# Attention, feed-forward and soft mixture-of-experts on one core: weight loads on a second queue, and a new order of the first sixteen tiles

## Chip, cores and metric

The kernel runs on 1 core of one Trainium2 chip. The metric is the device time of one execution in microseconds (us), shorter is better. The engines have short names: PE (TensorE matmul), PEld (its weight loads), DVE (VectorE), ACT (ScalarE), POOL (GpSimd), SP (SyncE, which here only issues DMAs).

## What is computed

The reference runs three stages over 4 batches of 768 positions (3072 tokens, 512 wide):

```python
# 1 local attention, 8 heads of 64, blocks of 32, window 16
k_sum = k.reshape(B, H, nb, block, D).max(axis=3)
v_sum = v.reshape(B, H, nb, block, D).mean(axis=3)
# scores against the near keys (masked) and against all k_sum (+ log(block)), one softmax over both
attn = softmax(concat(local, summary)) @ concat([v, v_sum])
# 2 feed-forward on x = attn, 3072 x 512, d_ff 2048
h = x @ w_in
x = (h * np.cos(h)) @ w_out
# 3 soft mixture of experts, 8 experts x 4 slots
logits = x @ phi
slot_input = softmax over tokens(logits).T @ x
out = softmax over slots(logits) @ (relu(slot_input @ w1) @ w2)
```

## The kernel before

**Tiles.** Stage 2 is a loop of 96 tiles, s = 0 to 95: 6 blocks of 512 tokens, each with 16 slices f = s % 16 of 128 hidden columns. Tile s does `mm1(s)` (lines 347 to 351: h = x·w_in in three passes of high and low parts), then the cosine (lines 365 to 372 on DVE, line 367 on ACT), the split of the product in a high part `gh` (line 375, ACT) and a low part `gl` (line 376, POOL), and two tiles later `mm2(s)` (lines 388 to 392). The low part of `w_in` (line 336, `wil`) is made by DVE for the first 16 slices and by POOL later; that of `w_out` (`wol`) always by POOL; both high parts (line 335) by ACT.

**Weights.** They come as 8-byte integers. In the first 16 tiles each slice is loaded once (`load_w`, line 113, 1 MB) and converted: `conv_1` (lines 123 and 127, ACT), `conv_2` (line 133, a shift on DVE), `conv_3` (line 138, an add on POOL). From f = 4 the load of slice f + 2 goes into the buffer which the conversion of slice f has just read.

**Attention.** Groups g = 0 to 3 are done before the tile loop; 4 to 7 fall into tiles 0 to 15, the others later. A group is: `att_K` (line 227, ACT copies the maxima of the keys in), `att_A` (line 250 PE scores `sc`, line 254 DVE scale and mask), `att_max` and `att_sub` (lines 262, 266), `att_exp` for two groups (line 271, ACT, with a load of another function table before it and one after it), `att_sum`, `att_norm` (lines 276, 290 to 293, DVE), `att_C` twice (line 300 PE transposes `tr`, line 306 copies `aT`), `att_D` (line 317 `av`, line 326). `HB` gives the half tile in which the groups of the second batch begin, (2, 13) for groups 4, 5 and 6, 7. The scores, transposes and value means of these groups share two PSUM banks (`ps_m`).

**Second batch's maxima and means.** Four loads of keys (`load_kraw`, line 162, buffer `kr`), each reduced by DVE (line 167, `ks`), and three of values (`load_vb`, line 174, `vb`), each averaged on PE (line 181, `vs`) and added by DVE (lines 190, 192), all through one buffer: each load waits for the reader of the one before. Load i stands at the end of tile i, its reader at the end of tile i + 1 (`at(i, 1, load)`, `at(i + 1, 1, use)`).

**Order.** Inside `manual_schedule` each engine runs its instructions in the order in which the code writes them. In a tile: mm1, lines 365 to 367, the attention pieces of position 0 (`fire(s, 0)`), lines 372 to 376, mm2 of tile s - 2, the low part for tile s + 2, the shift and add of slice s + 3 (`convert`, parts 2), the high and low part of `w_out`, `conv_1` of slice s + 4, the pieces of position 1. All DMAs are issued by SP, in this order too.

Of the kernel before, what the change touches and what calls it, by code (L numbers as in the profile page):

```python
# [12 lines left out]
I32 = mybir.dt.int32  # L13
# [13 lines left out]
KL = QB + 2 * WIN  # L27
NSUM = S // SUMB
KC = KL + NSUM
# [16 lines left out]
WARM1 = 4  # L46
WARM2 = 4
NRING = 7
HB = (2, 13)
HF = (-6, 10)  # L50
OA = 4
OV = 3
# [22 lines left out]
def body(ctx: ExitStack, tc: tile.TileContext, q0, qk, kT, vn, vx, w, phi, ex, cst, out):  # L75
    nc = tc.nc
# [30 lines left out]

    raw = {}

    def load_w(f):  # L110
        pool, tag, n = {2: (xres, "xl", 2), 3: (xres, "xh", 2)}.get(f, (m2, ("x2", "x2T")[f % 2], 1))
        raw[f] = pool.tile([128, 2, 512, 2], I32, name=f"raw{f}", tag=tag, bufs=n)
        return nc.sync.dma_start(out=raw[f].rearrange("p a c t -> p (a c t)"), in_=w[f].bitcast(I32))

    def conv_1(f, parts=(0, 1)):

# [14 lines left out]
    def conv_2(f):  # L131
        wi_ = W[f].rearrange("p a c -> p (a c)").bitcast(I32)
        nc.vector.tensor_single_scalar(out=wi_, in_=wi_, scalar=3, op=ALU.logical_shift_left)

    def conv_3(f):

        wi_ = W[f].rearrange("p a c -> p (a c)").bitcast(I32)
        return nc.gpsimd.tensor_tensor(out=wi_, in0=wi_, in1=cvt.pop(f), op=ALU.add)  # L138


    ksums, vsums, grp = {}, {}, {}
# [3 lines left out]
    def bank(name):  # L145

        pool, tag = banks[turns[0] % len(banks)]
        turns[0] += 1
        return pool.tile([128, 512], F32, name=name, tag=tag)
# [4 lines left out]
    def load_kraw(n):  # L154
        if n < 4:
            t = wres.tile([128, WIN + S + WIN], F32, name=f"kr{n}", tag=f"w{12 + n}")
            nc.gpsimd.memset(t[:, 0:WIN], 0.0)
            kfirst.append(t)
            t = t[:, WIN:WIN + S]
        else:  # L160
            t = att.tile([128, S], F32, name=f"kr{n}", tag="v2", bufs=1)
        nc.sync.dma_start(out=t, in_=kT[n])
        ksums[n] = t
# [30 lines left out]
    def vsum_first():  # L194

        ps = bank("vs0")
        for i in range(3):
            vsum_mm(ps, 0, i, i == 0, i == 2)
        vsums[0] = m2.tile([128, 4, 128], F32, name="vs0", tag="sacc")
        for p in range(4):  # L200
            nc.vector.tensor_copy(vsums[0][KL:KL + 32, p, :], ps[32 * p:32 * p + 32, 0:128])
# [11 lines left out]
    def load_v(g):  # L213
        pool, tag = {2: (wres, "w7"), 3: (att, "qk")}.get(g, (att, "v"))
        t = grp[g]["v"] = pool.tile([128, 2, 4, 128], F32, name=f"v{g}", tag=tag)
        nc.sync.dma_start(out=t.rearrange("p j w c -> p (j w c)"), in_=vx[g])

    def load_vs(g):
        p = 2 * (g % 2)
        for j in range(2):  # L220
            vs = vsums[0][KL:KC, p + j, :] if g < 6 else vsums[g // 6][32 * (p + j):32 * (p + j) + NSUM, :]
            nc.sync.dma_start(out=grp[g]["v"][KL:KC, j], in_=vs.unsqueeze(1).to_broadcast([NSUM, 4, 128]))
# [36 lines left out]
    def att_max(g, negate=False):  # L259
        d = grp[g]  # L260
        d["mx"] = stat.tile([128, 8], F32, name=f"mx{g}", tag="mx")
        nc.vector.tensor_reduce(out=d["mx"], in_=d["S"], axis=AX.X, op=ALU.max, negate=negate)
# [23 lines left out]
    def att_norm(g, eng=None):  # L286

        d = grp[g]
        sm = d["sm"]
        nc.vector.tensor_scalar(out=sm, in0=sm, scalar1=1e-9, scalar2=W_SCALE * TWO_PI, op0=ALU.add, op1=ALU.mult)  # L290
        rs = stat.tile([128, 8], F32, name=f"rs{g}", tag="rs")
        nc.vector.reciprocal(out=rs, in_=sm)
        (eng or nc.vector).tensor_tensor(out=d["S"], in0=d["S"],  # L293
                                         in1=rs.unsqueeze(2).to_broadcast([128, 8, KC]), op=ALU.mult)

    def att_C(g, j, eng=None):
        d = grp[g]
        ps = bank(f"tr{g}_{j}") if g < 4 else ps_m.tile([128, 512], F32, name=f"tr{g}_{j}", tag="m")
        for u in range(4):
            nc.tensor.transpose(ps[:KC, 128 * u:128 * u + 128], d["S"][:, 4 * j + u, :], ident)  # L300
        if g < 4:
            pool, tag, n = ring, ("gh", "gh", "gh", "gl", "gl", "gl", "a", "a")[2 * g + j], 2 if g == 3 else 3
        else:
            pool, tag, n = att, "aT", 2
        aT = pool.tile([KC, 512], F32, name=f"aT{g}_{j}", tag=tag, bufs=n)
        (nc.vector.tensor_copy if eng is nc.vector else nc.scalar.copy)(aT, ps[:KC, :])
        d["aT", j] = aT

    def att_D(g):
        d = grp[g]  # L310
        ps = bank(f"av{g}") if g < 4 else ps_m.tile([128, 512], F32, name=f"av{g}", tag="m")
        for j in range(2):
            for u in range(4):
                c = 256 * j + QB * u
                for hh in range(2):
                    r = slice(64 * hh, 64 * hh + 64)
                    product = nc.tensor.matmul(ps[r, c:c + QB], d["v"][:KC, j, u, r],  # L317
                                               d["aT", hh][:, 256 * j + QB * u:256 * j + QB * u + QB], start=True, stop=True)
        b, o = g // 4, 256 * ((g // 2) % 2)
        if b not in xh:  # L320
            xh[b] = xres.tile([128, 4, TB], F32R, name=f"xh{b}", tag="xh", bufs=2)
            xl[b] = xres.tile([128, 4, TB], F32R, name=f"xl{b}", tag="xl", bufs=2)
        p = 2 * (g % 2)
        ps = ps.rearrange("p (j c) -> p j c", j=2)
        hi, lo = (x[b][:, p:p + 2, o:o + 256] for x in (xh, xl))
        return product, nc.scalar.copy(hi, ps), nc.vector.tensor_tensor(out=lo, in0=ps, in1=hi, op=ALU.subtract)  # L326
# [174 lines left out]
    def at(s, pos, fn, *a):  # L501
        bg.setdefault((s, pos), []).append((fn, a))
# [12 lines left out]
    def fill(n):  # L515

        for i in range(n):
            nc.tensor.matmul(warmth[:, 0:128], ones, ones, start=True, stop=True)
# [4 lines left out]
    def scores(g):  # L523
        att_A(g)
        att_max(g, True)

    def turn(g, eng=None):
        for j in range(2):
            att_C(g, j, eng or nc.vector)
# [37 lines left out]
    att_norm(2, nc.gpsimd)  # L567
    scores(3)
    vsum_first()
    for g in (0, 2, 1, 3):  # L570
        load_vs(g)
    load_w(2)
    load_qk(4)
    load_w(3)
    att_exps(3)
    att_norm(1, nc.gpsimd)
    fill(8)
    turn(0)
    fill(6)
    conv_1(0)  # L580
    load_w(4)
    conv_1(1)
    load_w(5)
    turn(2)
    att_norm(3, nc.gpsimd)
    fill(8)
    turn(1)
    conv_2(0)
    conv_3(0)
    att_D(0)  # L590
    fill(4)
    turn(3, nc.scalar)
    att_D(2)
    split_w(0, 0, nc.vector)
    conv_2(1)
    conv_3(1)
    att_D(1)
    att_D(3)
    load_qk(5)
    load_v(4)  # L600
    load_v(5)
    load_vs(4)
    load_vs(5)
    split_w(1, 0, nc.vector)
# [5 lines left out]
    def convert(f, parts):  # L610
        if 1 in parts and f < NF:
            conv_1(f)
            if 4 <= f < NF - 2:
                load_w(f + 2)
        if 2 in parts and f < NF:
            conv_2(f)
            conv_3(f)


    for g in range(4, 24):  # L620
        h0 = HF[g // 2 % 2] + 2 * NF * (g // 4 - 1) if g > 7 else HB[g // 2 % 2]
        h = h0 + OA * (g % 2)
# [20 lines left out]
        else:  # L643
            v = n - 14 + OD2
# [15 lines left out]
    for b in range(1, B):  # L660
        s = 8 * (3 * b - 2) - 4
        for i in range(7):
            load, use, k = (load_kraw, ksum, (4 * b + i,)) if i < 4 else (load_vb, vsum, (b, i - 4))
            if b == 1:
                at(i, 1, load, *k)
                at(i + 1, 1, use, *k)
            else:
                at(s - 22 + 2 * i, 1, load, *k)
                at(s - 20 + 2 * i, 0, use, *k)
# [28 lines left out]
    for s in range(NSLOT + LAG):  # L698
        if s < NSLOT:
            mm1(s)  # L700
            if s == 0:
                convert(2, (2,))
            act1(s)
        fire(s, 0)
        if s < NSLOT:
            act2(s)
        if s >= LAG:
            mm2(s - LAG)
            if (s - LAG) % NF == NF - 1:
                last = [x2_out(t) for t in range(4)][3]  # L710
        if s == 0:
            convert(3, (1,))
        if s + 2 < NSLOT:
            split_w((s + 2) % NF, 0, nc.vector if s + 2 < NF else None)
        convert(s + 3, (2,))
        if s < NSLOT:
            split_w(s % NF, 1)
        convert(s + 4, (1,))
        fire(s, 1)
        fire(s, 2)  # L720
        if s - LAG >= NSLOT - NF:
            grab(wres, f"w{s - LAG - (NSLOT - NF)}")
# [129 lines left out]
    for h in range(2):  # L852
        c = slice(256 * h, 256 * h + 256)
# [22 lines left out]
        for i in range(NB):  # L876
            pool, tag, kw = places[(NB * h + i) % 4]
            o = pool.tile([128, 4, 256], F32, name=f"o{h}_{i}", tag=tag, **kw)
            for t in range(2):
# [3 lines left out]
                for n in range(2):  # L883
                    k = 512 * (i % 2) + 256 * t + 128 * n
# [78 lines left out]
```

## Time and profile before

| | us |
|---|---|
| time, median of 2 runs | 805.51 (805.39 to 805.64) |
| the profiled execution's own time | 806.3 |
| its span in the trace | 804.5 |

The profile gives, for each engine, when each instruction started, how long it ran, and how long the engine stood idle before it, with what released it. Times in the rows count from the span's start. In what follows a tile is dated by the start of its first DVE instruction, line 365.

### The profile page before, as it was taken

How to read it: one execution, taken by the hardware profiler on the slowest of the kernel's cores; microseconds unless marked ns; L12 is line 12 of the kernel's file. 1: busy time of each engine (PE TensorE's matmuls, PEld its weight loads, DVE VectorE, ACT ScalarE, POOL GpSimd, SP SyncE). 2: the span in 40 equal slices, each digit the busy share in tenths (PEclk: the TensorE clock that was granted, in tenths of full speed). 3: DMA queues.
4: the chain of work that ended last, by engine and by line, in shares of the span. 5: the costliest groups of instructions: out<-in, count | busy, mean ns of one | idle time of the engine just before them, and what ended most of it. 6: DMA issues, size and time to landing. Idle time of an engine off the chain costs nothing.

```text
span 804.5 us, 13755 instructions
## 1 busy us (share of the span) xinstructions
PE 735.0 (91%) x5453; PEld 567.9 (71%) x5453; DVE 476.4 (59%) x692; ACT 395.3 (49%) x703; POOL 412.3 (51%) x304
## 2 busy tenths in 40 slices
PE   8878477768999999999999999999999999999994
PEld 7756356656787788777777776887777888877453
DVE  6557664676656757757566567566576444443623
ACT  5675644733643645545436436455454453633212
POOL 2457454643556565555656565655457676672000
PEclk9999778969999999999999999999999999999998
DMA  9876534304212031041130220210100842227988
GB/s 339 293 271 245 185 143 182 108 20 136 81 50 89 1 115 63 21 141 70 58 106 1 65 76 1 96 43 28 36 1 27 317 155 79 89 94 270 378 313 269
DMA packets 36304, 101.71 MB, mean 126 GB/s; under 512 B 3472, under 2 KB 14736, under 8 KB 34192
## 3 DMA queue, kind: packets, MB, share of 16 engines
q1 hardware_dynamic: 36240, 100.83, 35.3%
q8 instruction: 43, 0.70, 0.4%
q14 instruction: 21, 0.17, 0.1%
HBM read 92.17 MB, written 6.29 MB: 122 GB/s over the span
## 4 chain that ended last, share of the span: by engine, by line
PE 67%; DVE 15%; ACT 7%; DMA 7%; issue 3%; SPq 1%; DVEq 0%; ACTq 0%
PE acc L388 9%; PE h L347 9%; PE h L348 8%; PE acc L389 8%; PE h L351 8%; PE acc L392 8%; DVE S L293 3%; DMA kr<-in_kT_dram 3%; PE av L317 3%; PE tr L300 2%; PE sc L250 2%; DVE a L366 2%; DVE a L365 2%; PE yp L861 2%; ACT S L271 2%
## 5 line engine op out<-in xcount | busy, mean ns | idle before, releaser
L376 POOL TENSOR_TENSOR gl<-a,gh 128x512 fp32r<-128x512 f32 x96 | 125.4, 1306 | 258.2 <-ACT gh L375 228.6
L367 ACT ACTIVATE a<-a,halfpi 128x512 f32<-128x512 f32 x96 | 69.5, 724 | 220.2 <-DVE a L366 211.5
L347 PE MATMUL h<-xh,wih 128*128 128x512 f32 x384 | 160.8, 419 | 5.2 <-ACT wih L335 5.1
L388 PE MATMUL acc<-woh,gh 128*128 128x512 f32 x384 | 159.0, 414 | 1.7 <-ACT gh L375 1.7
L389 PE MATMUL acc<-wol,gh 128*128 128x512 f32 x384 | 153.2, 399 | 3.5 <-POOL wol L336 3.5
L348 PE MATMUL h<-xl,wih 128*128 128x512 f32 x384 | 155.1, 404 | 0.6 <-DVE xl L326 0.6
L365 DVE TENSOR_SCALAR a<-h 128x512 f32<-128x512 f32 x96 | 65.9, 686 | 111.4 <-PE h L351 104.1
L336 POOL TENSOR_TENSOR wol<-w,woh 128x512 fp32r<-128x512 f32 x96 | 130.2, 1356 | 1.4 <-ACT woh L335 1.4
L336 POOL TENSOR_TENSOR wil<-w,wih 128x512 fp32r<-128x512 f32 x80 | 111.8, 1398 | 1.0 <-ACT wih L335 1.0
L375 ACT CAST gh<-a 128x512 fp32r<-128x512 f32 x96 | 59.4, 619 | 95.6 <-DVE a L372 95.5
L351 PE MATMUL h<-xh,wil 128*128 128x512 f32 x384 | 104.8, 395 | 0.0
L392 PE MATMUL acc<-woh,gl 128*128 128x512 f32 x384 | 103.3, 391 | 0.0
L388 PEld LDWEIGHTS acc<-woh,gh 128*128 128x128 f32 x384 | 73.4, 191 | 26.8 <-issue 9.4
L347 PEld LDWEIGHTS h<-xh,wih 128*128 128x128 f32 x384 | 74.8, 195 | 23.8 <-ACT wih L335 6.2
L372 DVE TENSOR_TENSOR a<-h,a 128x512 f32<-128x512 f32 x96 | 65.8, 686 | 39.4 <-ACT a L367 39.4
L389 PEld LDWEIGHTS acc<-wol,gh 128*128 128x128 f32 x384 | 73.6, 192 | 19.7 <-POOL wol L336 4.8
L348 PEld LDWEIGHTS h<-xl,wih 128*128 128x128 f32 x384 | 75.1, 196 | 16.1 <-DVE xl L326 1.0
L351 PEld LDWEIGHTS h<-xh,wil 128*128 128x128 f32 x384 | 72.9, 190 | 17.0 <-POOL wil L336 0.8
L392 PEld LDWEIGHTS acc<-woh,gl 128*128 128x128 f32 x384 | 72.3, 188 | 16.3
L366 DVE SCALAR_TENSOR_TENSOR a<-a,h 128x512 f32<-128x512 f32 x96 | 65.9, 687 | 3.3
L335 ACT CAST woh<-w 128x512 fp32r<-128x512 f32 x96 | 59.2, 616 | 3.0 <-PE acc L392 3.0
L335 ACT CAST wih<-w 128x512 fp32r<-128x512 f32 x96 | 59.1, 616 | 2.6 <-POOL w L138 2.6
(128 smaller groups left out, 879.0 us busy)
## 6 DMA issues: line engine op xcount, KB each, us to landing
ex<-in_ex_dram SPq DMA_DIRECT2D x64, 512.0 KB
raw<-in_w_dram SPq DMA_DIRECT2D x16, 1024.0 KB
qk<-in_qk_dram SPq DMA_DIRECT2D x20, 736.0 KB
v<-in_vx_dram SPq DMA_DIRECT2D x24, 512.0 KB
kr<-in_kT_dram SPq DMA_DIRECT2D x16, 384.0 KB
vb<-in_vn_dram SPq DMA_DIRECT2D x12, 512.0 KB
out_dram<-o SPq DMA_DIRECT2D x12, 512.0 KB
v<-vs SPq DMA_DIRECT2D x48, 48.0 KB
```

The costliest lines, as they stand in the source:

```text
L335: nc.scalar.copy(hi, W[f][:, part, :])
L336: (eng or nc.gpsimd).tensor_tensor(out=lo, in0=W[f][:, part, :], in1=hi, op=ALU.subtract)
L347: nc.tensor.matmul(h, hi[:, c], xh[s // NF][:, t, :], start=t == 0, stop=False)
L348: nc.tensor.matmul(h, hi[:, c], xl[s // NF][:, t, :], start=False, stop=False)
L351: nc.tensor.matmul(h, lo[:, c], xh[s // NF][:, t, :], start=False, stop=t == 3)
L365: nc.vector.tensor_scalar(out=a, in0=h, scalar1=0.25, scalar2=MAGIC, op0=ALU.add, op1=ALU.add)
L366: nc.vector.scalar_tensor_tensor(out=a, in0=a, scalar=MAGIC, in1=h, op0=ALU.subtract, op1=ALU.subtract)
L367: nc.scalar.activation(a, a, AF.Sin, bias=halfpi, scale=-TWO_PI)
L376: nc.gpsimd.tensor_tensor(out=gl, in0=a, in1=gh, op=ALU.subtract)
L388: nc.tensor.matmul(acc[t], gh[:, c], hi, start=f == 0, stop=False)
L389: nc.tensor.matmul(acc[t], gh[:, c], lo, start=False, stop=False)
L392: nc.tensor.matmul(acc[t], gl[:, c], hi, start=False, stop=f == NF - 1)
```

## The change

- `load_w` takes an engine. The loads of slices 4 and up are issued by ACT, right behind the conversion that frees their buffer; those of slices 2 and 3 move ahead on SP.
- `HB` becomes (1, 13): groups 4 and 5 come half a tile earlier; 6 and 7 stay.
- The first `load_kraw` of the second batch stands before the tile loop; the other loads move from position 1 to position 0 of the same tile, the readers from position 1 to 0 of theirs.
- In tiles 1 and up the shift and add of slice s + 3 stand ahead of the low part for tile s + 2. In tile 0 the high part of slice 2 stands ahead of the conversion of slice 3.
- Before the loop, the shift and add of slice 1 stand right behind those of slice 0, and DVE copies the first batch's means for groups 0 and 2 into their values (`copy_vs`) where a DMA did (line 222). Groups 1 and 3 keep the DMA. One `fill` has 6 matmuls for 8.

```diff
-HB = (2, 13)
+HB = (1, 13)
-    def load_w(f):
+    def load_w(f, eng=None):
-        return nc.sync.dma_start(out=raw[f].rearrange("p a c t -> p (a c t)"), in_=w[f].bitcast(I32))
+        return (eng or nc.sync).dma_start(out=raw[f].rearrange("p a c t -> p (a c t)"), in_=w[f].bitcast(I32))
...
+    def copy_vs(g):
+        p = 2 * (g % 2)
+        vs = vsums[0][KL:KC, p:p + 2, :]
+        nc.vector.tensor_copy(grp[g]["v"][KL:KC], vs.unsqueeze(2).to_broadcast([NSUM, 2, 4, 128]))
...
-    for g in (0, 2, 1, 3):
+    load_w(2)
+    load_w(3)
+    for g in (1, 3):
         load_vs(g)
-    load_w(2)
     load_qk(4)
-    load_w(3)
     att_exps(3)
     att_norm(1, nc.gpsimd)
+    copy_vs(0)
...
     conv_1(0)
-    load_w(4)
+    load_w(4, nc.scalar)
     conv_1(1)
-    load_w(5)
+    load_w(5, nc.scalar)
     turn(2)
     att_norm(3, nc.gpsimd)
-    fill(8)
+    copy_vs(2)
+    fill(6)
     turn(1)
     conv_2(0)
     conv_3(0)
+    conv_2(1)
+    conv_3(1)
...
-    conv_2(1)
-    conv_3(1)
...
     load_v(5)
+    load_kraw(4)
...
-                load_w(f + 2)
+                load_w(f + 2, nc.scalar)
...
             if b == 1:
-                at(i, 1, load, *k)
-                at(i + 1, 1, use, *k)
+                if i:
+                    at(i, 0, load, *k)
+                at(i + 1, 0, use, *k)
...
-        if s == 0:
-            convert(3, (1,))
+        if s:
+            convert(s + 3, (2,))
         if s + 2 < NSLOT:
             split_w((s + 2) % NF, 0, nc.vector if s + 2 < NF else None)
-        convert(s + 3, (2,))
+        if s == 0:
+            convert(3, (1, 2))
```

**DVE, tile 1.** `a1` is tile 1's cosine, `S4` the scores of group 4, `mx` and `ks` a maximum of scores and one of keys, `w4` the shift of slice 4, `wil3` the low part for tile 3. Before:

```order
L365 TENSOR_SCALAR a1_682<-h1_669 128x512
L366 SCALAR_TENSOR_TENSOR a1_682<-a1_682,h1_669 128x512
L254 SCALAR_TENSOR_TENSOR S4_686<-sc4_0_687,mask_85 128x480
L254 SCALAR_TENSOR_TENSOR S4_686<-sc4_1_688,mask_85 128x480
L372 TENSOR_TENSOR a1_682<-h1_669,a1_682 128x512
L336 TENSOR_TENSOR wil3_713<-w3_647,wih3_712 128x512
L133 TENSOR_SCALAR w4_661<-w4_661 128x1024
L262 TENSOR_REDUCE mx4_728<-S4_686 128x8
L167 TENSOR_REDUCE ks4_733<-kr4_667 128x24
L365 TENSOR_SCALAR a2_750<-h2_737 128x512
```

With the change (line 254 of group 4 now stands in tile 0):

```order
L365 TENSOR_SCALAR a1_699<-h1_686 128x512
L366 SCALAR_TENSOR_TENSOR a1_699<-a1_699,h1_686 128x512
L262 TENSOR_REDUCE mx4_703<-S4_665 128x8
L167 TENSOR_REDUCE ks4_708<-kr4_603 128x24
L372 TENSOR_TENSOR a1_699<-h1_686,a1_699 128x512
L133 TENSOR_SCALAR w4_659<-w4_659 128x1024
L336 TENSOR_TENSOR wil3_720<-w3_649,wih3_719 128x512
L365 TENSOR_SCALAR a2_748<-h2_735 128x512
```

The two reductions went from the tile's end into its middle, and the shift from behind the low part to before it.

**ACT, tile 6.** `aT4_0` is the copy of group 4's first transposes out of PSUM. Before:

```order
L375 CAST gh6_1022<-a6_1011 128x512
L335 CAST wih8_1038<-w8_920 128x512
L335 CAST woh6_1044<-w6_787 128x512
L123 ACTIVATE w10_1048<-raw10_924 128x1024
L127 ACTIVATE cv10_1050<-raw10_924 128x1024
L367 ACTIVATE a7_1106<-a7_1106,halfpi_90 128x512
L306 COPY aT4_0_1115<-tr4_0_1110 120x512
```

With the change:

```order
L375 CAST gh6_1034<-a6_1013 128x512
L335 CAST wih8_1052<-w8_921 128x512
L335 CAST woh6_1056<-w6_787 128x512
L123 ACTIVATE w10_1060<-raw10_925 128x1024
L127 ACTIVATE cv10_1062<-raw10_925 128x1024
L113 DMA raw12_1064<-in_w_dram 128x2048
L306 COPY aT4_0_1071<-tr4_0_1066 120x512
L367 ACTIVATE a7_1109<-a7_1109,halfpi_90 128x512
```

A weight load stands in ACT's row, and the copy now comes before the next tile's cosine. On PE the scores of group 6 come right behind the transposes `tr4_0` in the new order.

## Rows read from the trace of the kernel before

**Rows 1.** Stretches: us, busy (instructions) of PE, PEld, DVE, ACT, POOL, PEclk, DMA share, GB/s.

```profile
42.00:204.00 162.00, 118.21 (x771) 91.58 (x771) 100.86 (x128) 83.56 (x122) 87.39 (x52) 0.84 0.44 159
204.00:740.00 536.00, 529.42 (x3458) 415.95 (x3459) 324.18 (x466) 270.30 (x467) 312.54 (x238) 1.00 0.23 77
```

**Rows 2.** Timeline of PE (start, us, instruction, idle before it): three long waits.

```profile
89.12 1.08 PE L181 MATMUL vs<-vb,avg 128*32 128x128 f32 x16 [8.23 <-DMA vb<-in_vn_dram]
...
106.59 1.08 PE L181 MATMUL vs<-vb,avg 128*32 128x128 f32 x16 [8.13 <-DVE S L254]
...
128.82 2.11 PE L250 MATMUL sc<-qk 64*64 64x120 f32 x32 [3.92 <-ACT aT L306]
```

**Rows 3.** Timeline of DVE: all of tile 3, up to the start of tile 4.

```profile
67.98 0.68 DVE L365 TENSOR_SCALAR a<-h 128x512 f32<-128x512 f32 x1
68.70 0.69 DVE L366 SCALAR_TENSOR_TENSOR a<-a,h 128x512 f32<-128x512 f32 x1
69.30 1.21 DVE L254 SCALAR_TENSOR_TENSOR S<-sc,mask 128x480 f32<-128x480 f32 x2
70.44 0.68 DVE L372 TENSOR_TENSOR a<-h,a 128x512 f32<-128x512 f32 x1
72.32 1.37 DVE L336 TENSOR_TENSOR wil<-w,wih 128x512 fp32r<-128x512 f32 x1 [1.21 <-ACT wih L335]
73.62 0.68 DVE L133 TENSOR_SCALAR w<-w 128x1024 int32<-128x1024 int32 x1
74.22 1.14 DVE L262 TENSOR_REDUCE mx<-S 128x8 f32<-128x960 f32 x1
...
76.14 0.68 DVE L365 TENSOR_SCALAR a<-h 128x512 f32<-128x512 f32 x1
```

**Rows 4.** Timeline of DVE: the starts of tiles 0, 7, 9 and 11.

```profile
41.97 0.68 DVE L365 TENSOR_SCALAR a<-h 128x512 f32<-128x512 f32 x1
...
112.09 0.69 DVE L365 TENSOR_SCALAR a<-h 128x512 f32<-128x512 f32 x1 [4.06 <-PE h L351]
...
135.62 0.69 DVE L365 TENSOR_SCALAR a<-h 128x512 f32<-128x512 f32 x1 [3.42 <-PE h L351]
...
151.88 0.68 DVE L365 TENSOR_SCALAR a<-h 128x512 f32<-128x512 f32 x1
```

**Rows 5.** Timeline of POOL: the adds of slices 0 and 1, before the loop.

```profile
28.05 2.37 POOL L138 TENSOR_TENSOR w<-w,cv 128x1024 int32<-128x1024 int32 x1 [0.98 <-ACT cv L127]
37.26 2.38 POOL L138 TENSOR_TENSOR w<-w,cv 128x1024 int32<-128x1024 int32 x1 [6.84 <-DVE w L133]
```

**Rows 6.** Timeline of DVE: two products of `att_norm`, POOL idle and POOL busy.

```profile
96.56 1.16 DVE L293 TENSOR_TENSOR S<-S,rs 128x960 f32<-128x960 f32 x1
...
102.89 3.08 DVE L293 TENSOR_TENSOR S<-S,rs 128x960 f32<-128x960 f32 x1
```

**Rows 7.** Timeline of ACT: table load, exponentials, a high part, a conversion.

```profile
82.86 1.28 ACT L271 ACT_TABLE_LOAD   x1
84.15 1.80 ACT L271 ACTIVATE S<-S 128x1920 f32<-128x1920 f32 x1
...
87.27 0.72 ACT L367 ACTIVATE a<-a,halfpi 128x512 f32<-128x512 f32 x1
...
89.79 0.61 ACT L335 CAST woh<-w 128x512 fp32r<-128x512 f32 x1
90.31 1.15 ACT L123 ACTIVATE w<-raw 128x1024 f32<-128x1024 f32 x1
91.37 1.18 ACT L127 ACTIVATE cv<-raw 128x1024 int32<-128x1024 uint32 x1
```

**Rows 8.** Timeline of SP: issues of a means' DMA and of a key load.

```profile
20.79 0.98 SPq L222 DMA_DIRECT2D v<-vs  x1
...
60.70 0.33 SPq L162 DMA_DIRECT2D kr<-in_kT_dram  x1
```

**Rows 9.** Timeline of DVE: the reduction that waited for that key load.

```profile
67.11 0.95 DVE L167 TENSOR_REDUCE ks<-kr 128x24 f32<-128x768 f32 x1 [0.49 <-DMA kr<-in_kT_dram]
```

## The prediction, as put on record before the changed kernel was run

> **What bounds the kernel now.** I first read the stretches [rows 1]. After 204 us PE is busy 529.42 of 536 us at a granted clock of 1.00; nothing in the change touches that part. From 42 to 204 us, in tiles 0 to 15, PE is busy 118.21 of 162 us, and the mean clock is 0.84: its lower level is 1.2 GHz, the upper 2.4. There lie 44 idle us and some slow ones, so only there can this change pay. The timeline of PE then shows who ends the idle time. Three waits alone make 20.3 us [rows 2]: 8.23 on a load of the second batch's values, 8.13 on DVE scaling scores out of PSUM, 3.92 on ACT copying a transpose out of PSUM. None is PE's own, so I read DVE, which has all these tiles' work in one row.
>
> DVE's tile 3 [rows 3] takes 8.16 us from line 365 (67.98) to line 365 of tile 4 (76.14). Its steps, start to start: 1.32 for lines 365 and 366, 1.14 for the scores' scale, 1.88 from line 372 to the low part (of it 1.21 idle for ACT's high part), 1.30 for the low part, 0.60 for the shift, 1.92 for both reductions. PE would need less: 536 us for tiles 16 to 95 is 6.7 per tile, attention included [rows 1]. So the first sixteen tiles go at the pace of DVE's row and of what it waits for, and I price the change tile by tile on that row, then look where PE is later than DVE. Tiles 0, 4, 7, 9 and 11 start at 41.97, 76.14, 112.09, 135.62 and 151.88 [rows 3, 4].
>
> **Before the loop.** POOL's add of slice 1 starts at 37.26 after 6.84 idle, put down to DVE's shift, which stands behind the first low parts [rows 5]. With the shift right behind that of slice 0, the add can follow the first add, which started at 28.05 and took 2.37. Two new copies on DVE delay both. The trace has no such copy. For one, a shift over as many columns gives 0.60 from below, a product held up by POOL 3.08 from above [rows 3, 6]; I take 1.3, nearer the shift, since the copy too has one input. So the add of slice 1 starts at 28.05 + 2.6 + 2.37 = 33.0, and everything up to tile 0 hangs on it: 4.2 us gained; by the bounds 0.7 to 5.7.
>
> **ACT's loads.** No DMA is issued by ACT before. SP's issues take 0.33 for a load and 0.98 for the small means' DMA [rows 8]; I take 0.4, nearer the load, and nothing below zero, since ACT works in order. Twelve make 4.8 us on ACT, which counts only where somebody waits for ACT's tail: tiles 2 and 6 below, inside their sums. In exchange SP's key loads no longer stand behind weight loads. One before took from 60.70 to 67.11, 6.4 us [rows 8, 9]; I take 4.5 and keep 6.4 as the upper bound, and a gain from there is hidden except in tile 2.
>
> The Trainium skill (DMA: Bandwidth & Descriptors, "Issuing engines are not separate DMA queues") speaks against this part: transfers issued by different engines share the same DMA engines, and a second issuer saves only issue time. By it the key loads would keep their 6.4 us and the sum below would be some 2 us smaller; no row before shows two issuers at work.
>
> **Tiles 0 to 3** (34.17 us now). The shift now falls into the 1.21 that DVE waits for ACT, so a plain tile loses 0.60. The cosine needs a table load (1.28) and 0.72 in tile 0 [rows 7].
> - Tile 0: 1.32 + 1.28 + 0.72 + 1.88 + 1.30 + 0.60 + 1.14 (group 4's scale, now here) = 8.2.
> - Tile 1: 1.32 + 1.92 + 1.88 + 1.30 = 6.4. The keys' maxima no longer wait, since their load went out before the loop.
> - Tile 2: ACT's row decides. Behind tile 1's high part come a cast (0.52), the conversion (2.24), the load (0.4), group 5's two key copies (some 0.9, an estimate from two casts) and the cosine 0.72: 4.8, where DVE needs 1.30 + 1.32 + 0.95. So 1.3 of waiting: 1.32 + 0.95 + 1.3 + 1.88 + 1.30 + 1.14 = 7.9. PE's scores of group 5 wait for the same copies; that is hidden behind DVE.
> - Tile 3: 6.4 like tile 1.
>
> Sum 28.9: 5.3 gained.
>
> **Tiles 4 to 6** (35.95 now). Here the earlier attention only moves work.
> - Tile 4: the exponentials now stand before the high part `gh`: 1.32 + 0.72 + 1.28 + 1.80 + 1.04 (two casts) + 1.30 = 7.5.
> - Tile 5: the cosine's table 1.28 and 0.72, then at the end the first `att_norm`. It meets POOL's add, so I price it 3.0, not 1.16 [rows 6]: 1.32 + 2.0 + 1.88 + 1.30 + 0.4 + 3.0 + 1.1 = 11.0. PE's wait on the values (8.23 now) shrinks and lies beside this.
> - Tile 6: DVE's second product (1.16 and small pieces) brings line 372 to an end at 3.9. Then PE's scores of group 6, which stand right behind the transposes `tr4_0`, need that transpose's bank, whose copy is at the end of ACT's tile: three casts 1.56, conversion 2.24, load 0.4, copy 0.6 (as a cast of as many columns) = 4.8. From there to the next tile 6.8, as from 128.82 to 135.62 now [rows 2, 4]: after such a wait PE runs scores and mm1 at the lower clock. 15.5. So the 8.13 wait on DVE goes, and a new one on ACT comes.
>
> Sum 34.0: 2.0 gained.
>
> **Tiles 7 and 8** (23.53 now). Group 5's second transpose and the scores of group 7 no longer stand in one position, so the 3.92 wait and the slow clock behind it should go. Tile 7: 7.0, PE's pace. Tile 8: 1.32 + cosine 0.72 + cast 0.61 + line 326 0.7 (as line 372, on as many columns) + maximum 0.95 [rows 9] + 1.88 + 1.30 + 1.14 = 8.6. 7.9 gained.
>
> **Tiles 9 to 12** lose the shift's 0.60 each: 2.4 gained. Groups 6 and 7 keep their tiles, so the later waits stay.
>
> Together 4.2 + 5.3 + 2.0 + 7.9 + 2.4 = 21.8 us. From the profiled execution's own 806.3 (span 804.5 and 1.8 around it) that gives 784.5; the two timed runs have their median 0.8 lower, so I forecast 783.7. The rest is bound by PE and only shifts.
>
> **Rivals.**
> - *Holding ACT (slower).* Each ACT load first waits for an earlier transfer on the same semaphore, and ACT works in order. If it were held for a whole landing, 6.4 us less 3 (ACT is busy 83.56 of 162 us, 5.2 of each tile's 10.1, and tiles get shorter), ten tiles cost 34 us: 806.3 - 21.8 + 34 = 818. It decides once a load is held for over 5.2 us. Against it: the earlier transfer is mostly issued two or more tiles before. For it: in front of the loop the weights' loads follow closely on others.
> - *The pieces collide again.* The time that tile 8 loses comes back, since PE reaches the moved scores before ACT's copies, and tile 6 stays at 17: 793. For it speaks that every one of the long waits in rows 2 is of this kind; against it the order of PE, where tile 8's last copy now stands before a whole mm2.
> - *Two queues share the engines.* Key loads stay at 6.4 and weights come later: 2 to 4 us less, 787. By the page named above this is the expected case.
> - *Late tiles eat it.* Tiles 11 to 15 wait for something of fixed pace, a transfer or POOL, and give 10 us back: 794. Against it: the DMA share there is low, 0.44 over the whole stretch [rows 1].
> - *Better than that.* The product in tile 5 misses POOL (-1.9), tile 6 keeps the upper clock (-3), the copies cost 0.6 (-1.4): 777.
>
> **Chances.** My forecast 0.47, better 0.12, two queues 0.13, collision 0.15, late tiles 0.08, holding ACT 0.05. The likeliest case alone spans 779 to 789. Collision and late tiles reach 794; the copies' upper bound (3.5 us) on top gives 797, and 772 takes in the better case with the largest gain before the loop. So 772 to 797. A difference of 2%, about what a measurement of this kernel can tell from no change, lies at 789.4: faster 0.68, same 0.29, slower 0.03.
>
> **What would show it.** In the new profile: line 365 of tile 0 near 37.8; tile 4 near 66.7, tile 7 near 100.7, tile 9 near 116, tile 11 near 131; ACT issuing loads in under 0.5 each; the scores of group 6 waiting for ACT's `aT`; no wait of PE on DVE's line 254. Wrong would be: tile 0 after 41, waits of ACT's loads on a DMA of over 2 us each, or PE waiting over 3 us in tile 8.

## The result, and the profile after

The changed kernel takes 796.44 us (796.04 to 796.85) against 805.51: ratio 0.9887, 95% interval 0.9845 to 0.993. I had forecast 783.7. The gain is 9.1 us, not 21.8, and lies below the 2% at which the forecast drew the line between faster and no change.

The stretches, columns as in [rows 1]:

```profile
42.00:204.00 162.00, 129.87 (x839) 100.83 (x836) 115.57 (x140) 93.75 (x133) 95.51 (x55) 0.89 0.46 158
204.00:740.00 536.00, 527.96 (x3545) 413.87 (x3543) 324.48 (x480) 267.87 (x470) 308.96 (x235) 1.00 0.25 84
```

From 42 to 204 us PE now does 68 more instructions, at a mean granted clock of 0.89 against 0.84; tile 16 starts at 193.62 us and not at 203.46. Behind that nothing has changed, as expected. To see where the rest is I dated each tile by line 365, as before, and set it beside the sums of the forecast (span; before, forecast, after, in us):

| piece | before | forecast | after | missed by |
|---|---|---|---|---|
| up to tile 0 | 41.97 | 37.8 | 45.83 | 8.0 |
| tiles 0 to 3 | 34.17 | 28.9 | 28.55 | -0.3 |
| tiles 4 to 6 | 35.95 | 34.0 | 35.13 | 1.1 |
| tiles 7 and 8 | 23.53 | 15.6 | 16.30 | 0.7 |
| tiles 9 and 10 | 16.26 | 15.1 | 16.13 | 1.0 |
| tiles 11 to 15 | 51.58 | 50.4 | 51.68 | 1.3 |
| from tile 16 on | 601.04 | 601.0 | 601.48 | 0.4 |

Two thirds of the miss lies in one piece, in front of the loop. The forecast's mark "tile 0 after 41" for a wrong step came true. Here is that piece in the timeline of all engines of the changed kernel (start, us, instruction, idle before it and what ended it):

```profile
15.17 1.74 SPq L113 DMA_DIRECT2D raw<-in_w_dram  x2
...
25.82 3.58 SPq L222 DMA_DIRECT2D v<-vs  x4
27.09 0.38 ACTq L113 DMA_DIRECT2D raw<-in_w_dram  x1
27.52 1.17 ACT L123 ACTIVATE w<-raw 128x1024 f32<-128x1024 f32 x1 [1.59 <-DMA v<-in_vx_dram]
29.79 0.34 ACTq L113 DMA_DIRECT2D raw<-in_w_dram  x1
30.32 5.01 POOL L138 TENSOR_TENSOR w<-w,cv 128x1024 int32<-128x1024 int32 x2 [0.69 <-DVE w L133]
37.20 1.12 PE L317 MATMUL av<-aT,v 120*64 120x64 f32 x16 [5.00 <-DMA qk<-in_qk_dram]
39.55 1.76 PE L317 MATMUL av<-aT,v 120*64 120x64 f32 x28 [1.23 <-DMA v<-vs]
40.72 0.59 ACT L326 CAST xh<-av 128x512 fp32r<-128x512 f32 x1 [7.04 <-PE av L317]
45.83 0.69 DVE L365 TENSOR_SCALAR a<-h 128x512 f32<-128x512 f32 x1 [0.53 <-PE h L351]
```

The first row is the loads of slices 2 and 3. POOL's two adds ran back to back from 30.32, and the first took 2.71, so the second started near 33.0, as forecast. But tile 0 does not hang on it alone. PE stands still for 5.00 and 1.23 us in `av` of group 1, once in front of each half of its 32 matmuls; its means still come by DMA (line 222), and group 3, ACT and tile 0 stand behind it. The first wait is put down to the queries' DMA, which stands next to the means' on the same queue; but `av` reads the values with their means, and no queries. ACT's first load was held too: of the 1.59 us in the row behind it, ACT stood idle for 1.16 in front of the issue, put down to a load of values.

The stretches in front of the loop, first of the kernel before, then of the changed one:

```profile
26.00:32.00 6.00, 3.56 (x42) 3.23 (x41) 2.40 (x4) 2.51 (x3) 3.44 (x2) 0.73 0.40 72
32.00:38.00 6.00, 5.76 (x113) 4.95 (x112) 2.96 (x6) 3.25 (x6) 0.74 (x1) 0.99 0.99 412
```

```profile
26.00:32.00 6.00, 6.00 (x99) 5.59 (x97) 5.24 (x10) 3.81 (x5) 3.91 (x2) 1.00 1.02 391
32.00:38.00 6.00, 1.00 (x23) 0.89 (x18) 2.86 (x2) 1.21 (x2) 3.33 (x2) 0.87 1.04 321
```

Before, the small DMAs were issued from 20.79 to 30.05 us, the later ones while the DMA engines were 0.40 busy, and the bulk loads came behind them, from 30.09. Now the engines are full all along, and from 32 to 38 us PE is busy for 1.00 of 6 us. Tiles 4 to 6, in the timeline:

```profile
81.95 1.08 PE L181 MATMUL vs<-vb,avg 128*32 128x128 f32 x16 [4.14 <-DMA vb<-in_vn_dram]
...
88.57 2.86 POOL L138 TENSOR_TENSOR w<-w,cv 128x1024 int32<-128x1024 int32 x1
89.08 2.38 DVE L290 TENSOR_SCALAR sm<-sm 128x8 f32<-128x8 f32 x1
91.39 1.30 POOL L336 TENSOR_TENSOR wol<-w,woh 128x512 fp32r<-128x512 f32 x1
91.73 1.98 DVE L293 TENSOR_TENSOR S<-S,rs 128x960 f32<-128x960 f32 x1
...
103.18 1.87 PE L250 MATMUL sc<-qk 64*64 64x120 f32 x30 [4.66 <-ACT aT L306]
```

The values' wait fell from 8.23 to 4.14 [rows 2] and lies beside DVE's work. The new wait on ACT's `aT` in tile 6 is there as forecast. Tile 5 holds a surprise: an operation on 128 x 8 numbers takes 2.38 us. It starts in POOL's add and ends within 0.03 us of it.

### The profile page after: what moved, and what is told of

Its sections match the earlier page's. It is cut to its first block, busy times and chain, and to the rows that moved or that the text cites. A ratio compares the mean times of both kernels' runs of the same rounds, so it can differ in the third digit from the quotient of the medians.

```text
span 795.1 us, 13731 instructions
## 1 busy us (share of the span) xinstructions
PE 733.4 (92%) x5449; PEld 567.1 (71%) x5449; DVE 485.9 (61%) x694; ACT 395.7 (50%) x703; POOL 418.0 (53%) x304
## 4 chain that ended last, share of the span: by engine, by line
PE 66%; DVE 15%; ACT 9%; DMA 5%; issue 3%; POOL 1%; SPq 0%; ACTq 0%; DVEq 0%; POOLq 0%
PE acc L388 9%; PE h L347 8%; PE acc L389 8%; PE h L348 8%; PE acc L392 8%; PE h L351 8%; DVE S L293 3%; PE sc L250 2%; PE av L317 2%; PE tr L300 2%; DVE a L366 2%; DVE a L365 2%; PE yp L871 2%; DVE sm L290 2%; ACT S L271 2%
## 5 line engine op out<-in xcount | busy, mean ns | idle before, releaser
L347 PE MATMUL h<-xh,wih 128*128 128x512 f32 x384 | 157.7, 411 | 1.5 <-ACT wih L335 1.5
L389 PE MATMUL acc<-wol,gh 128*128 128x512 f32 x384 | 154.9, 403 | 4.2 <-POOL wol L336 4.2
L348 PE MATMUL h<-xl,wih 128*128 128x512 f32 x384 | 152.1, 396 | 0.0
L348 PEld LDWEIGHTS h<-xl,wih 128*128 128x128 f32 x384 | 73.3, 191 | 14.6
```

The costliest lines, as they stand in the source:

```text
L347: nc.tensor.matmul(h, hi[:, c], xh[s // NF][:, t, :], start=t == 0, stop=False)
L348: nc.tensor.matmul(h, hi[:, c], xl[s // NF][:, t, :], start=False, stop=False)
L389: nc.tensor.matmul(acc[t], gh[:, c], lo, start=False, stop=False)
```

## The experiments

All are edits of the changed kernel, timed beside the kernel before on the same chip, where that had medians of 805.70 to 806.88; so I compare runs by their ratios to it (0.001 is 0.8 us) and by the starts of line 365. Theory 1 blames the order on SP's queue for the late tile 0, theory 2 ACT's two loads of 1 MB each (slices 4 and 5), theory 3 the copies on DVE.

### The means first on SP's queue

```diff
-    load_w(2)
-    load_w(3)
     for g in (1, 3):
         load_vs(g)
+    load_w(2)
+    load_w(3)
```

> The changed kernel, with one thing other: on SP's queue the small means' DMAs of groups 1 and 3 stand ahead of the loads of slices 2 and 3, not behind them. Theory 1 (the order on SP's queue): the means wait behind two bulk loads; put first, they land before PE asks for them, PE's wait for v<-vs (1.23 us at 39.55) goes, tile 0 starts near 38 to 39 instead of 45.8, and the kernel takes about 789 us. Theory 2 (ACT's two loads of slices 4 and 5 take the DMA engines at 27 to 38 us): the order on SP hardly matters, tile 0 stays at 44 to 46, and the time at 795 to 797. Theory 3 (DVE's copies or POOL's adds set the start): no change either, 796, with PE waiting for DVE or POOL, not for a DMA, before tile 0.

794.11 us, ratio 0.9846 (0.9825 to 0.9866). Tile 0 starts at 39.27 as theory 1 says, but lasts 11.84 us for 8.45, and tile 2 8.47 for 6.93. The timeline of this run:

```profile
30.23 2.68 SPq L113 DMA_DIRECT2D raw<-in_w_dram  x2
32.30 0.34 ACTq L113 DMA_DIRECT2D raw<-in_w_dram  x1
32.73 0.58 ACT L326 CAST xh<-av 128x512 fp32r<-128x512 f32 x1 [3.41 <-DMA v<-vs]
32.95 2.89 SPq L210 DMA_DIRECT2D qk<-in_qk_dram  x2
43.68 0.44 ACT L227 COPY qk<-ks 128x96 f32<-128x96 f32 x2 [4.83 <-DMA qk<-in_qk_dram]
46.19 0.69 DVE L372 TENSOR_TENSOR a<-h,a 128x512 f32<-128x512 f32 x1 [5.50 <-ACT a L367]
```

SP holds slices 2 and 3 back until it has issued the means: 30.23 for 15.17. Group 4's queries and keys stand behind them, ACT waits 4.83 us for these, and DVE for ACT's cosine. So the 789 us of theory 1 did not come, though its early tile 0 did. ACT's second load is held here as well: its conversion ended at 29.32, the issue came at 32.30, and the trace puts the wait down to the means' DMA.

### Group 4's queries and keys first, too

```diff
-    load_w(2)
-    load_w(3)
     for g in (1, 3):
         load_vs(g)
     load_qk(4)
+    load_w(2)
+    load_w(3)
```

> The changed kernel with group 4's queries and keys, too, ahead of the loads of slices 2 and 3 on SP's queue, and not the means alone. With the means alone in front, tile 0 came 6.6 us earlier and tile 1 gave 3.4 back, because ACT's copy of those keys waited 4.83 us for their DMA. If the bulk loads ahead of a small DMA are what delays it, tile 0 stays near 39, tile 1 falls back to 8.4 to 8.6 us and the time to 789 to 791. Rival: SP now waits at the keys' issue for their buffers, the loads of slices 2 and 3 come later, and tiles 1 to 3 wait for the weights: 793 to 797.

794.32 us, ratio 0.9845 (0.9818 to 0.9872). The lost 3.4 us, which the expectation puts in tile 1, lie between the starts of tiles 0 and 1; that stretch is back at 8.46, so the wait was for these loads. But tile 0 starts at 42.90, since now the weights are late:

```profile
41.14 1.12 ACT L123 ACTIVATE w<-raw 128x1024 f32<-128x1024 f32 x1 [4.43 <-DMA raw<-in_w_dram]
42.30 0.69 DVE L133 TENSOR_SCALAR w<-w 128x1024 int32<-128x1024 int32 x1 [3.89 <-ACT w L123]
```

The rival's time came out, though in tile 0 and not in tiles 1 to 3. With ACT's two loads beside it, each of the three orders on SP's queue made somebody late: the means, the queries and keys, or the weights.

### Slices 4 and 5 loaded by SP

```diff
-    load_w(4, nc.scalar)
+    load_w(4)
-    load_w(5, nc.scalar)
+    load_w(5)
```

> The changed kernel, with one thing other: the loads of slices 4 and 5 in front of the loop are issued by SP again, not by ACT. Theory 1 (order on SP): the small means still stand behind the loads of slices 2 and 3, so tile 0 stays at 44 to 46 us and the time at 795 to 797. Theory 2 (ACT's queue takes DMA engines): the DMA share at 27 to 38 us falls, the means land some 5 us earlier, tile 0 starts near 39 to 41 and the time is near 790. Theory 3 (copies on DVE): no change, 796.

790.07 us, ratio 0.98 (0.9775 to 0.9825), some 7 us under the changed kernel by the ratios, 6.5 in the profiled spans, as theory 2 says. Tile 0 starts at 38.50. One expectation failed: the share of the DMA engines did not fall (1.04 from 26 to 32 us, 1.00 from 32 to 38). What fell is what runs beside the means. The timeline:

```profile
25.92 3.58 SPq L222 DMA_DIRECT2D v<-vs  x4
30.12 1.48 SPq L113 DMA_DIRECT2D raw<-in_w_dram  x2
32.73 2.09 PE L317 MATMUL av<-aT,v 120*64 120x64 f32 x64 [1.11 <-DMA v<-vs]
```

The means are issued at the same time as in the changed kernel (25.82), and PE has them by 32.73 instead of 39.55. From there to tile 0 it takes 5.77 us for 6.28, beside a granted clock of 1.00 from 38 to 44 us for 0.56. The two loads are issued at 30.12, behind the means. Their 2 MB take some 5 us at the 391 GB/s of that stretch (an estimate), which covers most of the 6.8 us between. The Trainium skill (DMA: Bandwidth & Descriptors, "Issuing engines are not separate DMA queues") says that transfers of several issuers interleave on the same engines, and that a second issuer saves only issue time; this run agrees with the first.

Theory 1 is not refuted by this. In the run with the keys first, ACT's two loads are issued beside the means, at 26.50 and 29.17, but slices 2 and 3 behind them, and PE waits for the last of the means only here:

```profile
34.62 0.69 PE L317 MATMUL av<-aT,v 120*64 120x64 f32 x16 [0.32 <-DMA v<-vs]
```

So the means came some 5 to 7 us late only with two bulk loads ahead of them on their own queue and two beside them on the other.

### All means copied by DVE

```diff
-    for g in (1, 3):
-        load_vs(g)
...
     turn(1)
+    copy_vs(1)
     conv_2(0)
...
     conv_3(1)
+    copy_vs(3)
```

> The changed kernel, with the means of groups 1 and 3 copied by DVE too, as those of groups 0 and 2 are, so that no means' DMA stands in front of the loop. Theories 1 and 2 (the means' DMAs are late, whatever delays them): both waits are gone; what is left is the queries' DMA (5.00 us of waiting at 37.20) if the bulk loads delay that too. Tile 0 near 38 to 40 us and the time near 789 to 791; with the queries' wait left over, tile 0 near 42 and 793. Theory 3 (the copies on DVE hold up the start): two more copies of 0.7 us make tile 0 later still, 46 to 48, and the time 797 to 798.

790.43 us, ratio 0.9803 (0.9778 to 0.9827), with ACT's loads where they were. Theory 3 falls: with two more copies tile 0 starts at 38.60, and `av` waits for no DMA. Two copies took 0.69 us each, one 0.85, and one 2.76, beside POOL's add:

```profile
29.39 2.70 POOL L138 TENSOR_TENSOR w<-w,cv 128x1024 int32<-128x1024 int32 x1 [1.42 <-DVE w L133]
29.88 2.76 DVE L530 COPY v<-vs 24x1024 f32<-24x1024 f32 x1
38.60 0.69 DVE L365 TENSOR_SCALAR a<-h 128x512 f32<-128x512 f32 x1 [0.77 <-PE h L351]
```

So the two large DMA streams hurt those who wait for a small DMA: take away the stream beside it or the small DMA, and tile 0 comes 7.2 to 7.3 us earlier.

### All weight loads by SP, in the loop too

```diff
-                load_w(f + 2, nc.scalar)
+                load_w(f + 2)
```

with the two lines of "Slices 4 and 5 loaded by SP".

> The changed kernel, with all weight loads issued by SP, in front of the loop and in it; the rest as changed. Theory: what ACT's queue brought is only the late start, so with all on SP tile 0 starts near 38.5 as in the run that moved the two loads in front of the loop, the tiles behind keep their durations to 0.3 us, and the time is 789 to 791. Rival by the prediction: SP's key and value loads in the loop again stand behind weight loads, PE's wait for the values in tile 4 and the keys in tiles 1 to 3 come back (2 to 4 us), and the time is 792 to 795.

789.86 us, ratio 0.9798 (0.9775 to 0.982), beside 790.07 with ACT's queue in the loop: no difference. Tile 0 starts at 38.74. Tile 2 takes 8.89, with a wait for the second batch's keys, but so it does with ACT's loads (8.58). First this run, then the one with slices 4 and 5 alone on SP:

```profile
57.53 0.95 DVE L167 TENSOR_REDUCE ks<-kr 128x24 f32<-128x768 f32 x1 [2.30 <-DMA kr<-in_kT_dram]
```

```profile
57.01 0.95 DVE L167 TENSOR_REDUCE ks<-kr 128x24 f32<-128x768 f32 x1 [1.99 <-DMA kr<-in_kT_dram]
```

The second queue, the first thing that the change names, is worth nothing in the loop that these runs could tell, and costs some 7 us in front of it, as long as means come by DMA.

### Groups 4 and 5 half a tile later

```diff
-HB = (1, 13)
+HB = (2, 13)
```

> The changed kernel, with the second batch's groups begun half a tile later again, as in the kernel before; everything else as changed. If the 8.1 us that tiles 7 and 8 gained come from the groups' place (PE no longer stops for DVE's scale of the scores and ACT's copy of a transpose in tile 8), tiles 7 and 8 go back from 16.3 to about 23 us, tile 6 loses its wait for ACT's aT copy, and the time is 801 to 804 us. If the gain comes from earlier key and value loads and the shift instead, tiles 7 and 8 stay at 16 to 18 us and the time is 795 to 798.

801.30 us, ratio 0.9936 (0.9911 to 0.9961), some 4 us over the changed kernel, though the two intervals overlap; the tiles tell more. Tiles 7 and 8 take 24.71 us for 16.30, and PE's wait in tile 8 is back:

```profile
123.64 2.11 PE L250 MATMUL sc<-qk 64*64 64x120 f32 x32 [4.43 <-ACT aT L306]
```

Tiles 5 and 6 take 23.98 for 27.37, so the early groups cost 3.4 us there and bring 8.4 behind. Tile 6 loses its wait on `aT`, as expected, but PE waits 4.22 us there for DVE's line 254 instead. The step on tiles 7 and 8 was right.

### The shift behind the low part

```diff
-        if s:
-            convert(s + 3, (2,))
...
         if s == 0:
-            convert(3, (1, 2))
+            convert(3, (1,))
+        convert(s + 3, (2,))
```

> The changed kernel, with DVE's shift (and POOL's add behind it) in the loop behind the low part again, as in the kernel before; the rest as changed. By the prediction's term the shift in front fills the 1.21 us for which DVE waits for ACT's high part and saves 0.60 us in each plain tile: undone, tiles 1, 3, 4 and 9 to 12 are each 0.5 to 0.7 us longer and the kernel takes 799 to 801 us. By the rival that the shift costs as much in its new place (beside POOL it took 1.7 to 1.9 us in tiles 9 and 10), only tiles 0 to 3 get longer, tiles 9 to 12 stay at 16.1 and 19.7 us for two and two tiles, and the time is 796 to 798.

797.27 us, ratio 0.989 (0.9869 to 0.9912): within 1 us of the changed kernel. But tile by tile both theories are half right. Tiles 1 to 4, 10 and 12 are 0.35 to 0.60 us longer; tiles 5 and 11, with a normalisation on DVE, are 1.0 shorter each. (Tiles 11 and 12 of the changed kernel take 18.89; the 19.7 in the expectation is a slip of mine.) Tile 5 of this run:

```profile
91.12 0.16 DVE L290 TENSOR_SCALAR sm<-sm 128x8 f32<-128x8 f32 x1
91.28 2.40 POOL L138 TENSOR_TENSOR w<-w,cv 128x1024 int32<-128x1024 int32 x1 [1.23 <-DVE sm L290]
91.55 3.15 DVE L293 TENSOR_TENSOR S<-S,rs 128x960 f32<-128x960 f32 x1
```

With the shift ahead, POOL's add starts earlier and meets the small line 290 (2.38), and POOL's low part then meets the product (1.98); with the shift behind, the add meets the product alone (3.15). From line 290 to the product's end that is 4.63 and 3.58 us. So the early shift saves 0.35 to 0.60 us in these tiles, and gives it back where it moves POOL's add onto DVE's normalisation.

### Two steps that follow

Both have the means copied by DVE. The first has group 4's first transposes half a tile earlier:

```diff
-            at2(n, att_C, g, 0)
+            at2(n - (g == 4), att_C, g, 0)
```

> The kernel with all four groups' means copied by DVE, and beside that group 4's first transposes half a tile earlier, so that ACT's copy of them no longer stands behind its conversion when PE wants their bank for the scores of group 6. If PE's wait of 4.66 us for that copy in tile 6 is what makes the tile 14 us long, tile 6 falls to 9 to 10 us and the time to 784 to 787. Rival: PE waits for something else there (DVE's product in tile 5, or the copy is as late as before because the transposes themselves wait), tile 6 stays at 13 to 14 and the time at 790.

784.27 us, ratio 0.9725 (0.9698 to 0.9752). Tile 6 falls from 14.05 to 10.03: the wait on `aT` was what made it long, as the forecast had it. The second has group 4's normalisation half a tile earlier as well, in tile 5 between POOL's low part and its product:

```diff
-            at2(n + 1, att_norm, g)
+            at2(n + (g > 4), att_norm, g)
```

> As the run with the earlier transposes, and beside that group 4's normalisation half a tile earlier, where POOL rests between its low part and its product. The three operations took 2.37, 0.20 and 1.98 us beside POOL's add, and 0.17, 0.20 and 1.16 for the next group without it. If POOL holds them up, they fall to about 1.6 us together and lie in the 1.1 us for which DVE waits for the cosine: tile 5 falls from 12.6 to 9 to 10 us, and the time to 781 to 784. If their length is their own, tile 5 stays above 12 us and the time is as without this edit.

781.09 us, ratio 0.9683 (0.9659 to 0.9707). Tile 5 falls from 12.48 to 9.41, tile 6 to 8.44. Its rows:

```profile
80.13 1.29 POOL L336 TENSOR_TENSOR wol<-w,woh 128x512 fp32r<-128x512 f32 x1
80.34 1.12 DVE L290 TENSOR_SCALAR sm<-sm 128x8 f32<-128x8 f32 x1
81.72 1.16 DVE L293 TENSOR_TENSOR S<-S,rs 128x960 f32<-128x960 f32 x1
```

Line 290 again ends with POOL's instruction, now a short one, and the product runs alone in 1.16: 2.5 us for the three operations, not the expected 1.6. (Tile 0 starts at 41.05 here and at 38.88 in the run before, with no edit in front of it; among the runs with all means copied it scatters between 38.6 and 41.05.) The same for group 6 too (`n + g % 2` for `n + (g > 4)`):

> As the run with the copies, the earlier transposes and group 4's earlier normalisation, and beside that group 6's normalisation half a tile earlier in tile 11. Tile 11 shows the same three operations beside POOL's add (2.33, 0.20 and 1.96 us). By the theory that their place beside POOL costs the time, tile 11 falls from 12.06 to about 9.5 us and the time to about 778.5. Rival: the next tile waits for PE or ACT instead, and tiles 11 and 12 together keep 18.9 us: 781.

779.23 us, ratio 0.9669 (0.9641 to 0.9698). Tile 11 falls from 12.06 to 9.17, and tile 12 gives 1.1 back. Its interval overlaps that of the run before, so the last 2 us are seen in the trace and not in the time. Last, the same with slices 4 and 5 loaded by SP:

> As the run with both normalisations earlier, and the loads of slices 4 and 5 in front of the loop issued by SP. No means' DMA is left that they could delay, so by theories 1 and 2 nothing changes beyond the scatter of the start (tile 0 between 38.5 and 41): the same time to 2 us. If ACT's issues themselves (two of 0.33 to 0.47 us) hold up the start, tile 0 comes 0.5 to 1 us earlier.

779.66 us, ratio 0.9666 (0.9644 to 0.9688): no difference, so where nobody waits for a small DMA, ACT's two loads cost nothing that shows. By the ratios the version before it is 27 us faster than the kernel before, and 18 us faster than the changed one.

## Why the prediction was wrong

- **Before the loop: wrong, 8.0 of the 12.4 us missed in the span.** The step that failed is "everything up to tile 0 hangs on it", on the add of slice 1. The add came near the forecast 33.0, in part by luck, since the two copies took 1.4 us together and not 2.6; but `av` of group 1 hung on the means' DMAs until 39.55. The diff showed their order reversed against slices 2 and 3, and two more bulk loads from ACT beside them, and I costed only the issues of those loads (0.4 forecast, 0.33 to 0.38 measured). With the means' wait gone tile 0 starts at 38.5 to 38.6, near the 37.8 of that step: the sum was about right for the engines, and left out the DMAs.
- **The copies:** 0.69 us each in the changed kernel for 1.3 forecast, near the lower bound of 0.60; the 2.76 of the fourth copy in the experiment shows that the upper bound was real.
- **Two queues:** this rival had the right mechanism, in the wrong place and at about half the price (2 to 4 us for some 7). I looked for it in the loop, where it is nothing, and not in front of it, where the DMA engines are full.
- **Tiles 0 to 3:** right in the sum, 28.55 for 28.9, with errors that cancel: in tile 2 (6.93 for 7.9) DVE waited 0.34 us for ACT's cosine and not 1.3, and the other three took 0.1 to 0.3 longer each.
- **Tiles 4 to 6:** the wait on ACT came, tile 6 took 14.82 for 15.5. Tile 5 took 12.55 for 11.0: the normalisation beside POOL was priced 3.4 with its small pieces and took 4.63, since POOL held up two operations and not one.
- **Tiles 7 and 8:** right, 16.30 for 15.6, and shown by the run with the groups half a tile later.
- **Tiles 9 to 12:** "lose the shift's 0.60 each" held in tiles 10 and 12, against the run with the shift behind. Tile 11 lost 1.0 by the same move, as tile 5 did, and tile 9 gained only 0.05: beside POOL the shift takes 1.91 us there and the low part 1.79, against 1.79 and 0.69 with the shift behind, which gives back what the filled wait of 1.21 saved. That tile 9 got 0.5 longer than before goes, in the trace, with DVE's wait for ACT's `xh` (line 326), 1.26 us for 0.67; no run singles that out.
- **Holding ACT:** not in the loop, where ACT's loads followed the conversion within 0.03 us and their issues took 0.33 to 0.34 each. In front of it the mechanism is real: ACT was held for 1.16 us in the changed kernel, hidden behind PE's wait for the means (with the loads on SP, `av` of group 2 came only 0.57 earlier, at 30.47), and for 2.98 in the run with the means first.
- **Late tiles:** tiles 11 to 15 gave back 0.1 us, not 10. **The pieces collide again:** did not come, since tile 8 took 9.12 and tile 6 14.82, not 17.
- **The range:** 796.44 lies inside 772 to 797 by luck. The upper end came from the collision or the late tiles with the copies' upper bound on top, and none of the three came. The lower end does not come out of the stated terms: the better case is 777, and the largest gain before the loop takes 1.5 more off, mostly counted in it already.

## What to carry to other kernels

When bulk loads move to another queue, list the small DMAs that are under way at that time and who waits for them; the issue's own cost is the least of it, and beside a second stream a new order on the queue only chose who was late. A step that saves time on DVE also moves POOL's instructions, so look what on DVE will then run beside them, the tiny operations too. Where a tile is long, look for the other engine's rest inside it and move the disturbed piece there: with the earlier transposes that took tiles 5 and 6 from 26.63 us to 17.85.

## What the runs showed of the hardware

- A DVE operation of 128 x 8 numbers took 0.16 us alone, and 1.12 and 2.38 when it started in an instruction of POOL; each time it ended within 0.05 us of it. The product of 128 x 960 took 1.16 alone, and 1.98 and 3.15 beside POOL, and ended 1.02 us behind POOL's instruction both times. So what is added is set by what is left of POOL's instruction, and not by the size of DVE's. Not every DVE instruction pays: the 24 maxima of line 262 in the changed kernel took 1.14 to 1.15 each, also where POOL was busy throughout (at 69.19 us).
- The Trainium skill (SBUF — State Buffer, "Who interferes with whom") says that DVE and GpSimd share a port pair which only some DVE instructions need, and that whoever comes first holds it for a whole instruction while the other blocks fully. These rows agree.
- The means' four DMAs of 48 KB, issued from 25.8 to 25.9 us on behind 2 MB on their own queue, were there for PE at 32.73 us, or at 39.55 when another queue had 2 MB under way beside them. With those beside and none ahead, issued from 25.53 on, they were there at 34.62.
